# Selective attention followed by a hard-swish feed-forward: loading of the first pair, two mask tables and the second half's bias sums moved

## The chip, the cores and the metric

The kernel runs on one core of one Trainium2 chip. A core has a matrix engine (TensorE, PE in the profile, with its weight loads shown apart as PEld), a vector engine (VectorE, DVE), an activation engine (ScalarE, ACT), a general engine (GpSimd, POOL) and a queue engine (SyncE, SP). Each runs its own list of instructions in order, and they wait for each other through semaphores. Transfers between the main memory and the core's memory are issued by SP, ACT or POOL; only POOL's change the number type on the way.

The metric is the device time of one execution in microseconds, the median of several runs. Lower is better.

## The reference

Shapes: 8 batches, 8 heads, 576 tokens, head size 64, feed-forward width 2048.

```
scores = scale * q @ k^T                          # scale 1/8, per head
cum    = cumsum(max(s, 0))                        # s: one number per head and token
bias   = -(cum[:, None] - cum[None, :])
scores = where(causal, -1e9, scores + min(bias, 0))
attn   = softmax(scores);   x = attn @ v          # heads side by side: 4608 x 512
h      = x @ w_in                                 # 512 x 2048
g      = h * clip(h + 3, 0, 6) / 6
out    = g @ w_out                                # 2048 x 512, float32
```

## The kernel before, in words

**Pairs and slots.** The 64 heads are worked off as 32 pairs of one batch. The main loop runs over the pair `p`; a *slot* is one pass, and slots are counted here from 0, as `p` is. In slot `p` PE computes the scores of pair `p`, ACT the exponentials (L335), PE the product with V (`av`, L386), DVE the division (`norm`, L408 and L409); a transpose brings the result into `xT`. Between these pieces stand calls of `group()`: each puts in one group of four 512-column matmuls of the feed-forward, either of its first product (`m1`, L452, followed by ACT's relu L467 and DVE's L468) or of its second (`m2`, L479, after every fourth of which DVE L495 scales the output block). Up to slot 13 a string, `plan`, says which; after that first and second products alternate while inputs allow. Groups begin in slot 4.

**How q and k arrive.** PE needs them in fp16 with the head size on the partitions. There are two ways. For pairs that are not *flat* (1 to 10), POOL issues a transfer that converts to fp16 on the way (L115, one for q and one for k), PE transposes it (L234), and four copies put it in place (L251; for k the even tokens' copy is ACT's). For flat pairs (0, and 11 on) SP or ACT issues a plain float32 transfer (L120), an engine casts it (`cast_qk`, L183), and it is transposed by PE (pair 0: L227, copies L211) or by a transposing transfer (pairs 11 on: L266 in SP's queue, copies L211 by DVE). V comes as float32 by three transfers in SP's queue (L131, L135), and POOL casts it (L187, L188).

**Bias.** The bias of a pair is added inside the score product: four extra rows (64 to 67) of the transposed q and k hold the running sums of `s`, split in fp16 parts. The sums of the first 32 heads are made at the start (`cum1` to `cum6`: a DVE scan L645, casts and subtractions), those of the other 32 heads later. `load_aug(p)` (L143) moves the rows of pair `p` in place, two small transfers. Pair 0 can't wait for that: DVE's `pick` (L668) makes its rows, and PE adds them by extra products (L282, L327).

**Masks.** Pairs 0 to 7 are masked by a product with a table `shut`. From pair 8 on rows 68 to 127 of the transposed q and k hold a *staircase* table, and DVE takes a minimum (L337, L369). There are four q/k buffers; each gets its table once (`set_stair`, L594, one copy for each head): POOL does it in slots 6 and 7, ACT at the beginning of slots 8 and 9, for the pairs 10 and 11.

**Order.** The order is written out by hand: what stands first in the program is first on its engine. Buffers: scores two banks, `ph` two banks, P three, V raw two, V cast three, q/k four. POOL's and SP's transfers each take one of eight semaphores in turn, so that one of them can wait until the eighth before it has landed.

**The start.** SP and ACT issue the loads of `s`, SP issues q of pair 0 and then its V, ACT issues k. PE runs 16 products on zeros (L606, `warm`, NWARM), ACT casts q and k, PE transposes them, ACT and DVE copy them, PE runs 4 more products on zeros, and the scores of pair 0 begin. POOL builds the identity and `shut`, issues pair 1's transfers, then pair 2's, casts V of pair 0, issues pair 3's.

Of the kernel before, what the change touches and what calls it, by code (L numbers as in the profile page):

```python
# [18 lines left out]
def kernel(  # L19
# [10 lines left out]
    nc = tc.nc  # L30
# [7 lines left out]
    NP = NHEADS // 2  # L38
# [10 lines left out]
    NVRAW = 2  # L49
    VW = 66  # L50
    NROW = 1
    NWARM = (16, 4)

# [47 lines left out]
    toks = {}  # L103

    def flat(p):
        return p < 1 or p >= NPE

    def load_qk(p, i, eng=nc.sync):
        b, h0 = p // PPB, 2 * (p % PPB)
        src = (q, k)[i][b, h0 : h0 + 2]  # L110
        if not flat(p):
            if not i:
                tok = work.tile([128, 24 * D], F16, tag="tok", bufs=4, name="tok")
                toks[p] = tok[0:96].rearrange("p (i h e d) -> p i h e d", i=2, h=2, e=6)
            nc.gpsimd.dma_start(  # L115
                out=toks[p][:, i].rearrange("p h e d -> p h (e d)"),
                in_=src.rearrange("h (p e) d -> p h (e d)", e=6),
            )
        else:
            eng.dma_start(  # L120
                out=raws[p % NRAW].rearrange("p (i t d) -> p i t d", i=2, t=9)[:, i],
                in_=src.rearrange("h s d -> (h s) d").rearrange(
                    "(t p) d -> p t d", p=128
                ),
            )
# [40 lines left out]
    def fill(eng, ap, value):  # L166

        word = np.array([value, value], np.float16).view(np.float32)[0]
        eng.memset(ap.bitcast(F32), float(word))
# [387 lines left out]
    def load_s(n, engs):  # L557
# [3 lines left out]
            eng.dma_start(out=C[n][32 * r : 32 * (r + 1)], in_=heads)  # L561

    load_s(0, (nc.sync, nc.scalar, nc.sync, nc.scalar))
    load_qk(0, 0)
    load_qk(0, 1, nc.scalar)
    nc.scalar.preload_act_table_set("natural_log_exp_and_others")
    load_v(0, nc.sync)
    fill(nc.gpsimd, ident, 0.0)
# [6 lines left out]
        base=0,  # L575
        channel_multiplier=-1,
    )
    fill(nc.gpsimd, shut, 0.0)
    for c in (slice(0, 512), slice(512, 640)):
        w = 128 if c.start == 0 else 64  # L580
# [8 lines left out]
            channel_multiplier=-1,  # L589
        )  # L590

    def set_stair(i, copy):
        for hh in range(2):
            copy(  # L594
                out=qks[i][64:128, hh, :, 64 * hh : 64 * hh + 640].rearrange(
                    "p i (t c) -> p i t c", c=128
                ),
                in_=stair_sb[64:128, :, None, :].to_broadcast([64, 2, 5, 128]),
            )
# [15 lines left out]
    nc.vector.memset(bias3, 3.0)  # L615
    fill(nc.gpsimd, rows_of[0][:, 0, :], 1.0)
    fill(nc.gpsimd, rows_of[0][:, 1, SEQ:640], 0.0)
    fill(nc.gpsimd, qks[0][64:68, :, :, :], 0.0)
    for i in range(2):
        load_qk(1, i)  # L620
    for i in range(NQK):
# [11 lines left out]
        op=ALU.add,  # L633
    )
    nc.vector.tensor_scalar_mul(out=ident2, in0=ident, scalar1=2.0)

    def cum1(n, eng):
        C["p"] = work.tile([128, SEQ], F32, tag="spos", bufs=1, name="spos")
# [4 lines left out]
    def cum2(n):  # L643
        C["c"] = work.tile([128, SEQ], F32, tag="c8", bufs=1, name="c8")
        nc.vector.tensor_tensor_scan(  # L645
            out=C["c"], data0=one.to_broadcast([128, SEQ]), data1=C["p"], initial=0.0, op0=ALU.mult, op1=ALU.add
        )
# [5 lines left out]
    def cum4(n, eng):  # L653
        C["r"] = work.tile([128, SEQ], F32, tag="s_all", bufs=1, name="r1")
        hi = rows_of[n][64:128, 1, 0:SEQ]
        eng.tensor_tensor(
            out=C["r"][64:128], in0=C["c"][64:128], in1=hi, op=ALU.subtract
        )
# [28 lines left out]
        out=C["p"][:, 304:SEQ], in_=C[0][:, 304:SEQ], func=AF.Relu, scale=8.0  # L687
    )
    cum2(0)
    nc.scalar.copy(out=rows_of[0][0:32, 0, 0:SEQ], in_=C["c"][0:32])  # L690
    cast_qk(0, nc.scalar.copy)
    cum3(0, V)
    cum4(0, V)
    cum5(0, V)
    cum6(0, V)
    pick(0)
    transpose(0, 0, (nc.scalar.copy,) * 2)
    transpose(0, 1)
    warm(NWARM[1])
    for g in range(1, 2 * NROW):  # L700
        pick(g)
    load_aug(1, nc.sync)
    load_v(1, nc.sync)
    load_aug(2, nc.sync)
    for i in range(2):
# [12 lines left out]
    for p in range(NP):  # L718
        nxt = p + 1 < NP
        if NPE <= p + 3 < NP:  # L720
            for i in range(2):
                load_qk(p + 3, i)
        def qk_ahead():
            if PPB < p + 3 < NPE:
                for i in range(2):
                    load_qk(p + 3, i)

        if p == 1:
            load_aug(4, nc.gpsimd)
        elif p == 2:  # L730
            load_w_in(0)
            cast_v(2)
            qk_ahead()
            load_aug(5, nc.gpsimd)
        elif p == 3:
            cast_v(3)
            load_w_in(1)
            qk_ahead()
            load_aug(6, nc.gpsimd)
            cast_v(4)  # L740
        elif p:
            qk_ahead()
            if NPE <= p + 2 < NP:
                cast_qk(p + 2)
                crossbar_qk(p + 2)
            for fn, c in {
                4: ((I, 2),),
                5: ((I, 3),),
                6: ((U, 0), (U, 1), (U, 2), (U, 3)),
                7: ((U, 4), (U, 5), (U, 6), (U, 7)),  # L750
            }.get(p, ()):
                fn(c)
            if nxt:
                cast_v(p + 1)
            if p in (6, 7):
                set_stair((p + 2) % NQK, nc.gpsimd.tensor_copy)
            elif p in (8, 9):
                set_stair((p + 2) % NQK, nc.scalar.copy)
            if p == 4:
                load_aug(7, nc.gpsimd)  # L760
            elif 5 < p < NP - 2:
                load_aug(p + 2, nc.gpsimd)
        if p and p + 2 < NP:
            load_v(p + 2, nc.sync)
        if p == 2:
            nc.sync.dma_start(out=stair_sb, in_=stair_dram.ap())
        if p == 9:
            load_s(1, (nc.sync,) * 4)
            fill(nc.gpsimd, rows_of[1][:, 0, :], 1.0)
        if p == 10:  # L770
            cum1(1, nc.gpsimd)
        if p == 11:
            cum2(1)
            nc.gpsimd.tensor_copy(out=rows_of[1][0:32, 0, 0:SEQ], in_=C["c"][0:32])
        if p == 12:
            cum3(1, nc.gpsimd)
            cum4(1, nc.gpsimd)
        if p == 13:
            cum5(1, nc.gpsimd)
            cum6(1, nc.gpsimd)  # L780

        if p == NPROD + 1:
            x_done[0] = NPROD

        def get(i):
            if p + 1 < NPE:
                transpose(p + 1, i)
            elif nxt:
                spread(p + 1, i)

        if p < PPB:
            scores(p, 0, 0)
            scores(p, 0, 1)
            get(0)
            scores(p, 0, 2)
            corner(p)
            if p:
                av(p - 1, 1, 0)
                av(p - 1, 1, 1)
                norm(p - 1, 1)  # L800
            get(1)
            scores(p, 1, 0)
            scores(p, 1, 1)
            av(p, 0, 0)
            scores(p, 1, 2)
            if p:
                transpose_x(p - 1)
            av(p, 0, 1)
            norm(p, 0)
            continue  # L810

        if p == PPB:
            early[0] = False
            scores(p, 0, 0)
            av(p - 1, 1, 0)
            av(p - 1, 1, 1)
            norm(p - 1, 1)
            m1_begin(0, 0, NKC - 1)
            scores(p, 0, 1)
            transpose_x(p - 1)  # L820
            m1_begin(0, 1, NKC - 1)
            pt = transpose_in(p + 1, 0)
            transpose_out(p + 1, 0, pt, pars=(0,))
            group()
            transpose_out(p + 1, 0, pt, pars=(1,))
            scores(p, 0, 2)
            group()
        else:
            if p == NPROD:
                nc.vector.tensor_scalar(  # L830
                    out=masks, in0=shut, scalar1=65504.0, scalar2=None, op0=ALU.add
                )
            scores(p, 0, 0)
            get(0)
            group()
            scores(p, 0, 1)
            av(p - 1, 1, 0)
            if p >= NPE - 1:
                get(1)
            group()  # L840
            scores(p, 0, 2)
            av(p - 1, 1, 1)
            norm(p - 1, 1)
            group()
        corner(p)
        group()
        if p > NPE:
            x_done[0] = p - 1
        if p == PPB:
            get(1)  # L850
            av(p, 0, 0)
        scores(p, 1, 0)
        if PPB < p < NPROD:
            get(1)
        group()
        if NPROD <= p < NPE - 1:
            get(1)
        scores(p, 1, 1)
        if p != PPB:
            av(p, 0, 0)  # L860
        if PPB < p < NPROD:
            transpose_x(p - 1)
        elif p >= NPROD:
            crossbar_x(p - 1)
        group()
        scores(p, 1, 2)
        group()
        av(p, 0, 1)
        norm(p, 0)
        group()  # L870
# [3 lines left out]
    group()  # L874
    av(p, 1, 1)
    norm(p, 1)
    group()
    group()
    transpose_x(p)
# [31 lines left out]
```

## Time and profile before

| | |
|---|---|
| Median of 5 runs | 359.68 us (359.47 to 361.41) |
| The profiled execution | 360.13 us, of which its span (first to last instruction) is 358.3 |
| Granted TensorE clock | 0.999 |
| PE busy | 347.0 us, 97% of the span |
| DVE, ACT, POOL busy | 251.4, 224.9, 127.5 us |
| DMA engines, mean busy | about 1.0 to 1.2 in the stretch to 65 us, 0.1 to 0.2 after 260 us |

The profile names an instruction by engine, line, operation and operands. A row of the timeline gives start, duration, then what runs and how often; in brackets the engine's idle time before it and what ended that. Matmuls overlap, so that a row's duration is longer than the time to the next start: a group of four 512-column matmuls is shown as 1.03 us, and the next row starts 0.86 us after it. What a wait costs PE is read from starts.

### The profile page before, as it was taken

What the parts mean: (1) busy time and instruction counts of PE and PEld (TensorE: products, weight loads), DVE (VectorE), ACT (ScalarE), POOL (GpSimd) and SP (SyncE); (2) the same over time, 40 slices, a digit from 0 to 9 for tenths busy, and PEclk for the clock granted to TensorE, in tenths of its full rate; (3) what the DMA queues carried; (4) which work ended last, traced back from release to release, by engine and by line L of the source; (5) the groups of instructions that cost most, each with busy time, mean ns of one, the idle gap of its engine ahead of it and who ended that gap; (6) DMA issues with size and microseconds to landing.
All of it is one profiled execution on the core that took longest, in us unless ns stands there. A gap on an engine that the chain in (4) does not pass through costs nothing.

```text
span 358.3 us, 7729 instructions
## 1 busy us (share of the span) xinstructions
PE 347.0 (97%) x2920; PEld 191.7 (54%) x2920; DVE 251.4 (70%) x541; ACT 224.9 (63%) x390; POOL 127.5 (36%) x219
## 2 busy tenths in 40 slices
PE   8999998899999999999999999999999999999995
PEld 3776665555555555555555555555555444444442
DVE  7897997697998777786768776767665544545531
ACT  4897888788677666666666666666665344333410
POOL 8575976654674433434233524342000000000000
PEclk9999999999999999999999999999999999999999
DMA  9899999989999996979698959899320101101111
GB/s 172 142 196 175 181 195 199 186 186 177 208 209 170 234 186 162 202 168 183 158 164 197 202 130 203 155 208 148 72 77 20 59 2 59 59 2 59 59 58 63
DMA packets 146991, 50.88 MB, mean 142 GB/s; under 512 B 133624, under 2 KB 141992, under 8 KB 146952
## 3 DMA queue, kind: packets, MB, share of 16 engines
q1 hardware_dynamic: 135304, 42.13, 59.8%
q0 software_dynamic: 10240, 7.67, 13.9%
q10 hardware_dynamic: 1408, 0.57, 0.7%
q8 instruction: 23, 0.38, 0.4%
q14 instruction: 16, 0.13, 0.1%
HBM read 37.36 MB, written 9.44 MB: 131 GB/s over the span
## 4 chain that ended last, share of the span: by engine, by line
PE 84%; DVE 6%; DMA 4%; ACT 3%; issue 1%; POOL 1%; ACTq 0%; SPq 0%; DVEq 0%; POOLq 0%
PE po L479 33%; PE ph L452 32%; PE O L386 7%; PE S L316 7%; PE S L305 3%; DMA vraw<-in_v_dram 3%; ACT qk L594 1%; DVE gT L468 1%; DVE qk L251 1%; ACT P L335 1%; DMA s_all<-in_s_dram 1%; PE pt L234 1%; DVE qk L211 1%; ACT tr L467 1%; DVE x L409 1%
## 5 line engine op out<-in xcount | busy, mean ns | idle before, releaser
L468 DVE SCALAR_TENSOR_TENSOR gT<-tr,ph 128x512 f16<-128x512 f32 x144 | 98.9, 687 | 78.0 <-ACT tr L467 76.5
L452 PE MATMUL ph<-xT,w_in_sb 128*128 128x512 f16 x576 | 148.2, 379 | 0.3 <-DVE gT L468 0.2
L479 PE MATMUL po<-w_out_sb,gT 128*128 128x512 f16 x576 | 145.8, 379 | 0.3 <-DMA w_out_sb<-in_moe_w_out_dram 0.3
L467 ACT ACTIVATE tr<-ph,bias 128x512 f32<-128x512 f32 x144 | 99.0, 687 | 73.0 <-PE ph L452 71.5
L335 ACT ACTIVATE P<-S 128x512 f16<-128x512 f32 x192 | 111.5, 596 | 39.1 <-PE S L305 21.6
L452 PEld LDWEIGHTS <-w_in_sb 128*128 128x128 f16 x576 | 51.8, 97 | 44.7 <-issue 0.5
L479 PEld LDWEIGHTS <-gT 128*128 128x128 f16 x576 | 50.2, 98 | 46.5 <-issue 0.8
L316 PE MATMUL S<-qk 68*128 68x448 f16 (+3 forms) x256 | 48.9, 272 | 0.9 <-ACT P L335 0.9
L183 POOL CAST tok<-raw 128x576 f16<-128x576 f32 x42 | 28.2, 673 | 58.7 <-DMA raw<-in_q_dram 47.2
L386 PE MATMUL O<-va,P 128*128 128x65 f16 x896 | 47.8, 193 | 0.6 <-POOL va L187 0.6
L386 PEld LDWEIGHTS <-P 128*128 128x128 f16 x896 | 39.4, 97 | 14.4 <-issue 0.7
L187 POOL CAST va<-vraw 128x512 f16<-128x512 f32 x32 | 20.4, 638 | 56.7 <-DMA vraw<-in_v_dram 42.5
L316 PEld LDWEIGHTS <-qk 68*128 68x128 f16 x256 | 23.7, 98 | 24.9 <-issue 1.4
L143 POOL DMA_DIRECT2D qk<-rows_of x56 | 33.3, 597 | 3.5 <-PE S L305 2.5
L409 DVE TENSOR_TENSOR x<-O,rl 128x320 f16<-128x320 f32 x64 | 31.5, 492 | 2.2
L211 DVE COPY qk<-jt 64x768 f16<-64x768 f16 x84 | 31.3, 372 | 1.2
L495 DVE TENSOR_SCALAR ob<-po 128x512 f32<-128x512 f32 (+1 forms) x36 | 24.4, 678 | 9.5 <-PE po L479 8.9
L337 DVE TENSOR_TENSOR P<-P,shut 128x512 f16<-128x512 f16 x48 | 24.5, 511 | 5.6 <-ACT P L335 5.5
L305 PEld LDWEIGHTS <-qk 128*128 128x128 f16 (+1 forms) x256 | 18.9, 98 | 13.7 <-DVE qk L251 1.2
L251 DVE COPY qk<-pt 64x576 f16<-64x576 f16 x30 | 24.1, 804 | 3.0 <-PE pt L234 1.3
L305 PE MATMUL S<-qk 128*128 128x128 f16 (+1 forms) x256 | 25.0, 219 | 1.2 <-DVE rl L408 0.7
L386 PE MATMUL O<-va,PC 128*128 128x65 f16 x64 | 12.4, 193 | 0.8 <-DVE PC L369 0.8
(72 smaller groups left out, 174.4 us busy)
## 6 DMA issues: line engine op xcount, KB each, us to landing
out_dram<-ob SPq DMA_DIRECT2D x35, 256.0 KB, 2.0
vraw<-in_v_dram SPq DMA_DIRECT2D x64, 128.0 KB, 3.3
raw<-in_q_dram SPq DMA_DIRECT2D x22, 288.0 KB, 4.0
raw<-in_k_dram SPq DMA_DIRECT2D x21, 288.0 KB, 4.3
w_in_sb<-in_moe_w_in_dram POOLq DMA_DIRECT2D x4, 512.0 KB, 9.4
w_out_sb<-in_moe_w_out_dram POOLq DMA_DIRECT2D x8, 256.0 KB, 9.5
tok<-in_q_dram POOLq DMA_DIRECT2D x10, 144.0 KB, 5.2
tok<-in_k_dram POOLq DMA_DIRECT2D x10, 144.0 KB, 5.4
```

What stands on the lines that cost most here:

```text
L143: eng.dma_start(out=qks[p % NQK][64:68, hh, :, 64 * hh : 64 * hh + SEQ], in_=rows_of[g // 32].rearrange("(r g) i t -> g r i t", g=32)[g % ...
L183: copy(out=toks[p][:, c], in_=raws[p % NRAW][:, c])
L211: copies[par](out=qk[0:64, :, i, 128 * par : 128 * par + 256 * n].rearrange("p h (s two c) -> p h s two c", two=2, c=128)[:, :, :, 0, :], ...
L305: mm(S[:, c], lhsT=kT[rows, c], rhs=qT[rows, c], start=(j == 0 and not by_product), stop=(j == 3),)
L316: mm(S[:, c : c + w], lhsT=kT[0:68, 128 * j : 128 * (j + 1)], rhs=qT[0:68, 128 * (j + 1) : SEQ], start=(c == 0), stop=(c != 0 and p >= NROW),)
L335: nc.scalar.activation(out=pt[:, c], in_=S, func=AF.Exp, scale=0.125)
L386: mm(o[:, i, :], lhsT=lhsT, rhs=va[:, hh, j, 0:65], **kw)
L409: nc.vector.tensor_tensor(out=X[p][:, :, hh, :], in0=o[:, :, 0:64], in1=rl.to_broadcast([128, 5, 64]), op=ALU.mult,)
L452: mm(ph, lhsT=w_in_sb[:, kc, ft * 128 : (ft + 1) * 128], rhs=xT[:, kc, n * 512 : (n + 1) * 512], start=(kc == 0), stop=(kc == NKC - 1),)
L467: nc.scalar.activation(out=tr, in_=ph, func=AF.Relu, bias=bias3[:, 0:1])
L468: nc.vector.scalar_tensor_tensor(out=gTs[n][:, ft, :], in0=tr, scalar=6.0, in1=ph, op0=ALU.min, op1=ALU.mult)
L479: mm(po, lhsT=gTs[n][:, ft, t4 * 128 : (t4 + 1) * 128], rhs=w_out_sb[:, ft, :], start=(ft == 0), stop=(ft == NFT - 1),)
```

## The change

It has these parts.

1. Pair 0 is no longer flat: its q and k come by POOL's converting transfers, issued after the identity is built and before `shut`. The float32 transfers (one in SP's queue, one in ACT's) and ACT's two casts go. Its transposes are now twelve of 96 columns (L234) and its copies four of L251: ACT makes both of q and the even one of k, DVE the odd one of k. In ACT's order q's copies stand before the cast of the bias row (L690, now L692), k's behind it; in DVE's order k's copy stands between `pick(0)` and `pick(1)`.
2. NWARM goes from (16, 4) to (12, 10).
3. `load_aug(1)` moves from SP's queue to POOL's, ahead of pair 2's transfers and the cast of pair 0's V.
4. Half of a clearing of four partitions (L169 on `qk`) goes from POOL to DVE.
5. ACT's staircases of slots 8 and 9 are done one head at a time: the first after the corner, the second after the last scores of the slot. `load_aug(10)` and `load_aug(11)` go behind the second.
6. The second bias sums: the loads of `s` go from slot 9 to 12, `cum1` from 10 to 13, and `cum2` (the DVE scan) to `cum6`, in slots 11 to 13 before, all to slot 14, followed there by `load_aug(16)`.
7. One more `group()` before the transpose of the last pair.

```
-    NWARM = (16, 4)
+    NWARM = (12, 10)
     def flat(p):
-        return p < 1 or p >= NPE
+        return p >= NPE
     load_s(0, (nc.sync, nc.scalar, nc.sync, nc.scalar))
-    load_qk(0, 0)
-    load_qk(0, 1, nc.scalar)
     nc.scalar.preload_act_table_set("natural_log_exp_and_others")
     load_v(0, nc.sync)
...
+    for i in range(2):
+        load_qk(0, i)
     fill(nc.gpsimd, shut, 0.0)
...
-    def set_stair(i, copy):
-        for hh in range(2):
+    def set_stair(i, copy, heads=(0, 1)):
+        for hh in heads:
...
-    fill(nc.gpsimd, qks[0][64:68, :, :, :], 0.0)
+    fill(nc.gpsimd, qks[0][64:68, 1, :, :], 0.0)
...
     nc.vector.tensor_scalar_mul(out=ident2, in0=ident, scalar1=2.0)
+    fill(nc.vector, qks[0][64:68, 0, :, :], 0.0)
...
     cum2(0)
+    transpose(0, 0, (nc.scalar.copy,) * 2)
     nc.scalar.copy(out=rows_of[0][0:32, 0, 0:SEQ], in_=C["c"][0:32])
-    cast_qk(0, nc.scalar.copy)
     cum3(0, V)
     cum4(0, V)
+    pt = transpose_in(0, 1)
+    transpose_out(0, 1, pt, pars=(0,))
     cum5(0, V)
     cum6(0, V)
     pick(0)
-    transpose(0, 0, (nc.scalar.copy,) * 2)
-    transpose(0, 1)
+    transpose_out(0, 1, pt, pars=(1,))
     warm(NWARM[1])
     for g in range(1, 2 * NROW):
         pick(g)
-    load_aug(1, nc.sync)
+    load_aug(1, nc.gpsimd)
...
             if p in (6, 7):
                 set_stair((p + 2) % NQK, nc.gpsimd.tensor_copy)
-            elif p in (8, 9):
-                set_stair((p + 2) % NQK, nc.scalar.copy)
             if p == 4:
                 load_aug(7, nc.gpsimd)
-            elif 5 < p < NP - 2:
+            elif p in (6, 7) or 9 < p < NP - 2 and p != 14:
                 load_aug(p + 2, nc.gpsimd)
...
-        if p == 9:
+        if p == 12:
             load_s(1, (nc.sync,) * 4)
             fill(nc.gpsimd, rows_of[1][:, 0, :], 1.0)
-        if p == 10:
+        if p == 13:
             cum1(1, nc.gpsimd)
-        if p == 11:
+        if p == 14:
             cum2(1)
             nc.gpsimd.tensor_copy(out=rows_of[1][0:32, 0, 0:SEQ], in_=C["c"][0:32])
-        if p == 12:
             cum3(1, nc.gpsimd)
             cum4(1, nc.gpsimd)
-        if p == 13:
             cum5(1, nc.gpsimd)
             cum6(1, nc.gpsimd)
+            load_aug(16, nc.gpsimd)
...
         corner(p)
+        if p in (8, 9):
+            set_stair((p + 2) % NQK, nc.scalar.copy, (0,))
         group()
...
         scores(p, 1, 2)
         group()
+        if p in (8, 9):
+            set_stair((p + 2) % NQK, nc.scalar.copy, (1,))
+            load_aug(p + 2, nc.gpsimd)
         av(p, 0, 1)
         norm(p, 0)
         group()
...
     av(p, 1, 1)
     norm(p, 1)
     group()
+    group()
     group()
     transpose_x(p)
```

More of the change, by code (lines that the diff above doesn't have):

```diff
@@ L51 @@
     NROW = 1
-    NWARM = (16, 4)
+    NWARM = (12, 10)
     grp = (np.arange(128) * 61 // 128)[None, :]
@@ L105, in flat @@
     def flat(p):
-        return p < 1 or p >= NPE
+        return p >= NPE
     def load_qk(p, i, eng=nc.sync):
@@ L563 @@
     load_s(0, (nc.sync, nc.scalar, nc.sync, nc.scalar))
-    load_qk(0, 0)
-    load_qk(0, 1, nc.scalar)
     nc.scalar.preload_act_table_set("natural_log_exp_and_others")
@@ L577 @@
     )
+    for i in range(2):
+        load_qk(0, i)
     fill(nc.gpsimd, shut, 0.0)
@@ L590, with set_stair @@
         )
-    def set_stair(i, copy):
-        for hh in range(2):
+    def set_stair(i, copy, heads=(0, 1)):
+        for hh in heads:
             copy(
@@ L617 @@
     fill(nc.gpsimd, rows_of[0][:, 1, SEQ:640], 0.0)
-    fill(nc.gpsimd, qks[0][64:68, :, :, :], 0.0)
+    fill(nc.gpsimd, qks[0][64:68, 1, :, :], 0.0)
     for i in range(2):
@@ L635 @@
     nc.vector.tensor_scalar_mul(out=ident2, in0=ident, scalar1=2.0)
+    fill(nc.vector, qks[0][64:68, 0, :, :], 0.0)
     def cum1(n, eng):
@@ L689 @@
     cum2(0)
+    transpose(0, 0, (nc.scalar.copy,) * 2)
     nc.scalar.copy(out=rows_of[0][0:32, 0, 0:SEQ], in_=C["c"][0:32])
-    cast_qk(0, nc.scalar.copy)
     cum3(0, V)
     cum4(0, V)
+    pt = transpose_in(0, 1)
+    transpose_out(0, 1, pt, pars=(0,))
     cum5(0, V)
@@ L696 @@
     pick(0)
-    transpose(0, 0, (nc.scalar.copy,) * 2)
-    transpose(0, 1)
+    transpose_out(0, 1, pt, pars=(1,))
     warm(NWARM[1])
@@ L701 @@
         pick(g)
-    load_aug(1, nc.sync)
+    load_aug(1, nc.gpsimd)
     load_v(1, nc.sync)
@@ L756 @@
                 set_stair((p + 2) % NQK, nc.gpsimd.tensor_copy)
-            elif p in (8, 9):
-                set_stair((p + 2) % NQK, nc.scalar.copy)
             if p == 4:
                 load_aug(7, nc.gpsimd)
-            elif 5 < p < NP - 2:
+            elif p in (6, 7) or 9 < p < NP - 2 and p != 14:
                 load_aug(p + 2, nc.gpsimd)
@@ L766 @@
             nc.sync.dma_start(out=stair_sb, in_=stair_dram.ap())
-        if p == 9:
+        if p == 12:
             load_s(1, (nc.sync,) * 4)
             fill(nc.gpsimd, rows_of[1][:, 0, :], 1.0)
-        if p == 10:
+        if p == 13:
             cum1(1, nc.gpsimd)
-        if p == 11:
+        if p == 14:
             cum2(1)
             nc.gpsimd.tensor_copy(out=rows_of[1][0:32, 0, 0:SEQ], in_=C["c"][0:32])
-        if p == 12:
             cum3(1, nc.gpsimd)
             cum4(1, nc.gpsimd)
-        if p == 13:
             cum5(1, nc.gpsimd)
             cum6(1, nc.gpsimd)
+            load_aug(16, nc.gpsimd)
         if p == NPROD + 1:
@@ L845 @@
         corner(p)
+        if p in (8, 9):
+            set_stair((p + 2) % NQK, nc.scalar.copy, (0,))
         group()
@@ L867 @@
         group()
+        if p in (8, 9):
+            set_stair((p + 2) % NQK, nc.scalar.copy, (1,))
+            load_aug(p + 2, nc.gpsimd)
         av(p, 0, 1)
@@ L876 @@
     norm(p, 1)
+    group()
     group()
```

## The prediction

> **What bounds the kernel now.** I read the page first, then PE's waits, then the timeline around each.
>
> ```profile
> PE 347.0 (97%) x2920; PEld 191.7 (54%) x2920; DVE 251.4 (70%) x541; ACT 224.9 (63%) x390; POOL 127.5 (36%) x219
> PE 84%; DVE 6%; DMA 4%; ACT 3%; issue 1%; POOL 1%; ACTq 0%; SPq 0%; DVEq 0%; POOLq 0%
> ```
>
> PE is the bound, and the chain that ended last is PE for 84%. A gain can only come from PE's waits and from the start:
>
> ```profile
> PE S L316 <- ACT P L335: 0.9, 1, 0.9
> PE O L386 <- DVE PC L369: 0.8, 1, 0.8
> PE S L305 <- DVE rl L408: 0.7, 1, 0.7
> PE O L386 <- POOL va L187: 0.6, 1, 0.6
> PE po L479 <- DMA w_out_sb<-in_moe_w_out_dram: 0.3, 1, 0.3
> PE S L305 <- DVE qk L251: 0.3, 1, 0.3
> ```
>
> A matmul's drawn end hides a part of each wait, so I price them by starts, against the same pair of rows elsewhere: slot 4, V of pair 4, 30.68 to 31.73 where 24.25 to 24.50 is usual: 0.80 lost; slot 8, 60.04 to 61.39 against 78.23 to 78.48: 1.10; the w_out wait 0.49 (two matmuls take 0.92, not 0.43); scores of pair 9, 67.17 to 68.03 against 71.34 to 71.37: 0.83; scores of pair 10, 76.44 to 76.91: 0.44; slot 11, 90.84 to 91.97 against 95.52 to 95.70: 0.95; the last pair's transpose, 276.22 to 277.44 where a group takes 0.86: 0.36. Together 5.0 us: more is not to be had behind the start. The rows:
>
> ```profile
> 4.34 0.81 POOL L115 DMA_DIRECT2D tok<-in_q_dram  x1
> 8.62 0.60 DVE L668 TENSOR_SCALAR w_out_sb<-rows_of,sel 128x576 f16<-128x576 f16 x1
> 9.25 1.01 DVE L211 COPY qk<-pt 64x768 f16<-64x768 f16 x2
> 10.32 0.34 PE L305 MATMUL S<-qk 68*128 68x128 f16 x3 [0.22 <-DVE qk L211]
> 14.86 0.61 POOL L187 CAST va<-vraw 128x512 f16<-128x512 f32 x1 [4.28 <-DMA vraw<-in_v_dram]
> 31.73 0.41 PE L386 MATMUL O<-va,P 128*128 128x65 f16 x8 [0.63 <-POOL va L187]
> ...
> 58.31 2.41 ACT L594 COPY qk<-stair_sb 64x1280 f16<-64x1280 f16 x2
> 61.39 0.38 PE L316 MATMUL S<-qk 68*128 68x320 f16 x2 [0.95 <-ACT P L335]
> 66.56 0.59 PE L479 MATMUL po<-w_out_sb,gT 128*128 128x512 f16 x2 [0.32 <-DMA w_out_sb<-in_moe_w_out_dram]
> 68.03 0.38 PE L305 MATMUL S<-qk 128*128 128x128 f16 x4 [0.67 <-DVE rl L408]
> 76.91 0.40 PE L305 MATMUL S<-qk 128*128 128x128 f16 x4 [0.28 <-DVE qk L251]
> ...
> 86.36 1.35 DVE L645 TENSOR_TENSOR_SCAN c<-one,spos 128x576 f32<-128x576 f32 x1
> 91.97 0.20 PE L386 MATMUL O<-va,PC 128*128 128x65 f16 x1 [0.79 <-DVE PC L369]
> ```
>
> The first scores hang on DVE's queue; V's cast idled for 4.28 us for a load; the staircase on ACT stopped PE in slot 8; two waits on transfers follow it; the scan in slot 11 made DVE late.
>
> **The change part by part.** Shifts are PE's place against before.
>
> *Start.* POOL can issue q at 1.28 (identity done at 1.25) and k at 2.1 (0.81 and 0.68 each). Pair 1's transfers took 4.2 and 4.0 from issue to landing while the DMA engines were full (share 1.34 to 1.36 from 4 to 7 us), so q lands at 5.5, k at 6.1. PE's 12 products start 0.427 apart from 1.19: done at 6.3, and this decides. Transposes 0.42, so ACT starts at 6.7: q's two copies 1.6, bias row 0.67 (9.0), k's even copy 0.8 (9.8); DVE's odd copy, which waits for that, 0.81; scores at 10.6, against 10.32: +0.3. `pick(0)`, which now waits for ACT's row until 9.0, ends at 9.65 and fits before. PE's ten products (2.15) end before 9.1. The two casts (1.24) and two plain issues go, but ACT was not last. Bounds: DVE's own chain (8.62 + 0.60 + 0.81 = 10.0) gives -0.3; a landing as slow as the slowest later pair's (10.2) gives +3.9. I take +0.3, by the nearest rows in time. The half clearing on DVE (1.44 for all on POOL, so about 0.7) fits DVE's 1.13 idle before `s`.
>
> *V and POOL's queue.* SP no longer waits with pair 1's V behind the bias rows (8.75), so that V is there early, and POOL doesn't idle 4.28. From the row at 9.0 POOL has `load_aug(1)` 1.2, pair 2's transfers 1.3, V's cast 1.3 (done at 12.8; `av` needs it at 13.2 + 0.3), pair 3's 1.3, V's cast 0.9, pair 4's 1.25, two bias issues 1.2: the first w_in load goes out at 17.4, not 18.07. Pair 2's q lands at 10.2 + 3.4 = 13.6, needed at 14.7 + 0.3. Pair 4's V is held by the full DMA engines behind that load (share 1.1 to 1.25 from 18 to 32), so it lands some 0.65 earlier than 30.9; PE reaches it at 31.1 + 0.3 = 31.4 and waits no more: shift -0.3. Bounds: -0.8 (start unchanged, wait gone) to the start's whole loss.
>
> *Slot 8.* No staircase ahead of the exponentials: 1.10 gone. But the last w_out load (issued 57.74) landed 8.8 later, at 66.5, just when PE went on; pair 9's bias rows, behind it in POOL's queue (61.89, landing 6.0 later), at 67.9, and PE started pair 9 at 68.03. I put that wait down to them, not to the DVE row named. The DMA engines are full from 41 to 65 (share 1.2), so these landings move only with POOL's earlier work: 0.3 to 0.65, I take 0.45. Pair 9 starts at 67.6: the 1.10 is swallowed. Shift -0.45; -1.55 if the stream follows PE.
>
> *Slots 9 and 10.* The staircase no longer delays ACT's first exponential of pair 9 (69.36 becomes 68.4); losses of 0.2 twice (68.95, 72.46) go. But a half (1.25) now stands between the corner's exponential and pair 9's second head: ACT 72.6 to 73.8, then exponential, relu and k's copy (74.42 before) at 74.8 to 75.6, DVE's copy to 76.45, pair 10 at 76.5: shift -0.4. The other half stands at 77.2 to 78.4, ahead of pair 10's first exponential (77.34 before, now 78.35): its score banks come free late, for PE 0.1 and 0.25. Shift -0.1 after slot 10. Bounds: +1.5, if both halves of slot 9 reach PE almost whole (2 x 1.25 less 0.9), and -0.8, if neither does. The moved `load_aug(10)` and `(11)` now wait for ACT at about 67 and 78.4; behind them POOL holds the casts of pair 11's and 12's q and k, whose transposing transfers SP issued at 71.2 and 80.65. The second cast then ends near 81: a little late, covered until DVE reads it (88.3 before).
>
> *Slot 11.* The scan (1.35) goes, and the cast of POOL beside DVE's copy: -0.95, to -1.05. Bounds 0 to -0.95.
>
> *Slot 14.* There the scan is added, and five sums on POOL (0.68, 0.68, 1.28, 0.67, 1.28 in before's rows) with a clearing, waiting for the scan, and then `load_aug(16)`; behind them pair 17's cast. Pair 16 has a whole slot for it.
>
> ```profile
> 92.50:100.30 7.80, 7.80 (x74) 4.48 (x73) 7.64 (x17) 5.49 (x10) 5.66 (x10) 1.00 1.05 186
> 100.30:109.00 8.70, 8.70 (x82) 5.10 (x81) 8.51 (x19) 6.05 (x11) 6.22 (x9) 1.00 1.16 223
> 109.00:117.50 8.50, 8.50 (x79) 4.81 (x77) 6.26 (x15) 5.72 (x11) 3.28 (x6) 1.00 1.09 167
> ```
>
> These are slots 12 to 14: length, then busy PE, PEld, DVE, ACT, POOL. DVE has 2.2 of 8.5 us free in slot 14, more than 1.35; in slots 12 and 13, with the sums, it was full and PE lost nothing. I take +0.15; bounds 0 and 0.95, as in slot 11.
>
> DVE's two copies at 78.74 took 0.65 with POOL quiet, and at 89.81, beside POOL's cast at 89.73, 1.12. [...]
>
> *`s` loads and `cum1`* in slots 12 and 13: SP's four issues (2.04) and POOL's 2.15 move; POOL's casts waited 47.2 us in total for raw loads, so nothing for PE; if that cover is gone a cast is 2 us late, against a slot's slack. *Last `group()`*: 0.86 of ready work before the transpose; -0.35 (0 to -0.36).
>
> Sum: -0.1 - 0.95 + 0.15 - 0.35 = -1.25. The profiled execution took 360.13, 0.45 above the median 359.68: 358.9 in its terms, 358.4 as a median. A difference under about 0.3% (1.1 us) I count as none.
>
> **The rivals.**
>
> 1. *Slot 8's 1.10 is kept*, because the transfer stream runs earlier with PE: -1.1 more, 357.3. For: w_out's issues wait for landings that began with work PE releases. Against: share 1.2 for 24 us.
> 2. *Nothing is gained*: the halves reach PE in slots 9 and 10 (+0.6 on my figure) and the scan's loss only moves to slot 14 (+0.8): 359.8. For: DVE had no idle time from 70 to 77. Against: DVE's room in slot 14.
> 3. *Slower: pair 11's bias rows come too late.* Issued at 78.4 instead of 69.9, needed by its first scores at 84.4 less the shift. Landings of such rows took 2.4 to 8.4; over 6 it decides, and at 8.4 costs 2.4: 360.8. Against: 3.3 to 3.6 at that place before.
> 4. *Slower: pair 0 lands late*, as do later pairs with other loads beside them (8.4 at 19.65). k would be there at 10.5, scores 2.3 later; slot 4's wait and slot 8's spare 1.1 take up part if the transfers keep their time, else 2 remain: about 360.7. It decides from a landing of 6 or more.
>
> **How the numbers follow.** My forecast 0.48, rival 1 0.12, rival 2 0.20, rivals 3 and 4 0.10 each. The forecast lies just beyond the bound, with some 0.08 of its 0.48 within it. Faster: 0.40 + 0.12 = 0.52; same: 0.20 + 0.08 = 0.28, of which rivals' milder cases take no more; slower 0.20. The range goes from 356.8 (rival 1 with the start at -0.3) to 361.0 (rivals 3 and 4); for the likeliest case alone 357.6 to 359.2.
>
> **What would show it.** Scores of pair 0 at 10.6 with ACT's L251 from 6.7; POOL without an idle 4 us before pair 1's V; no POOL wait at `av` of slot 4; no ACT wait in slot 8 but a longer w_out wait and pair 9 at 67 to 68; an L305 wait at pair 10 and an ACT one in slot 10; no wait on L369 in slot 11; DVE full in slot 14. Wrong would be: transposes of pair 0 past 7, a wait on `qk` at pair 11, or a wait over 1 us in slot 14.

## The result: 0.7% slower

The changed kernel took 362.07 us as the median of 28 runs (360.74 to 366.01), against 359.91 for the kernel before (52 runs, 359.28 to 364.49). The medians lie 0.6% apart; the ratio of 1.0074, 95% interval 1.0053 to 1.0095, is that of the means (362.99 and 360.33), which the long runs raise. Ratios leave out runs more than 1.5% above the fastest of the same kernel; that concerns two of r1's twelve below. The profiled run took 360.74, span 358.9, against 360.13 and 358.3 before. So two things have to be explained: the profile is 0.6 us longer where 1.25 less was forecast, and the median lies another 1.3 above the profile.

The page and the waits of the changed kernel, in us in total, times, longest:

```profile
PE 346.6 (97%) x2924; PEld 192.0 (53%) x2924; DVE 250.8 (70%) x541; ACT 224.4 (63%) x389; POOL 128.8 (36%) x223
...
POOL qk L143 <- ACT qk L594: 12.7, 4, 4.8
PE ph L452 <- DVE gT L468: 4.2, 2, 2.6
PE S L305 <- DVE qk L251: 0.6, 1, 0.6
```

The waits of before on L335 in slot 8, L369 (slot 11), L187 (slot 4) and the `w_out` loads are gone from this list. Two new ones have come: PE waits 4.2 us for `gT`, in two places, and POOL stands 12.7 us behind ScalarE's staircases with bias rows to issue (L143).

First the kernel before in slots 9 and 10, POOL's casts and bias rows and DVE's masking (L337):

```profile
66.83 0.66 POOL L183 CAST tok<-raw 128x576 f16<-128x576 f32 x1 [1.75 <-DMA raw<-in_q_dram]
69.99 0.42 DVE L337 TENSOR_TENSOR P<-P,shut 128x512 f16<-128x512 f16 x1 [1.48 <-ACT P L335]
73.39 0.66 POOL L183 CAST tok<-raw 128x576 f16<-128x576 f32 x1 [1.96 <-DMA raw<-in_q_dram]
77.90 1.28 POOL L143 DMA_DIRECT2D qk<-rows_of  x2
```

The timeline of the changed kernel around slots 9 and 10 (start, length, engine, operation, in brackets the idle time before it and what ended it):

```profile
64.27 1.33 SPq L436 DMA_TRANSPOSE xT<-x  x1
65.78 0.38 PE L305 MATMUL S<-qk 128*128 128x128 f16 x4
67.35 0.57 POOL L143 DMA_DIRECT2D qk<-rows_of  x1 [3.10 <-ACT qk L594]
67.70 1.84 DVE L337 TENSOR_TENSOR P<-P,shut 128x512 f16<-128x512 f16 x1 [0.68 <-ACT P L335]
67.92 1.28 POOL L183 CAST tok<-raw 128x576 f16<-128x576 f32 x2
71.11 0.69 DVE L468 SCALAR_TENSOR_TENSOR gT<-tr,ph 128x512 f16<-128x512 f32 x1
71.85 1.02 PE L452 MATMUL ph<-xT,w_in_sb 128*128 128x512 f16 x4 [1.55 <-DVE gT L468]
...
77.85 0.57 POOL L143 DMA_DIRECT2D qk<-rows_of  x1 [4.79 <-ACT qk L594]
78.21 1.84 DVE L337 TENSOR_TENSOR P<-P,shut 128x512 f16<-128x512 f16 x1 [0.58 <-ACT P L335]
78.42 1.28 POOL L183 CAST tok<-raw 128x576 f16<-128x576 f32 x2
79.63 0.89 POOL L187 CAST va<-vraw 128x512 f16<-128x512 f32 x1
79.97 2.16 DVE L211 COPY qk<-jt 64x768 f16<-64x768 f16 x2
80.71 1.22 POOL L143 DMA_DIRECT2D qk<-rows_of  x2
82.91 1.02 PE L452 MATMUL ph<-xT,w_in_sb 128*128 128x512 f16 x4 [2.61 <-DVE gT L468]
```

Read each half from the top. POOL issues the second head's bias rows as soon as ScalarE has finished its staircase, and its casts follow at once. DVE's masking (L337) runs at that moment and takes 1.84 us; its next one, at 73.67, takes 0.42. In slot 10 the copies behind it (L211) take 2.16 instead of 0.65, beside POOL's cast of V and the next bias issues. `gT`, which stands behind them in DVE's queue, is late, and PE stops.

Where the time went is seen best from PE's place at the first scores of each pair, after against before: pair 0 10.50 against 10.32 (+0.2), pair 9 65.78 against 68.03 (-2.3), pair 10 75.60 against 76.91 (-1.3), pair 11 86.40 against 84.42 (+2.0), pair 12 93.90 against 92.88 (+1.0), and the end +0.6. The changed kernel is 2.3 us ahead at pair 9, gains 1.4 behind pair 11, and loses 4.2 in slots 9 and 10. Not all of the 2.3 is the change's: r11 below, the kernel before with one transfer moved, comes to pair 9 at 66.65, 1.4 earlier than the profile of before, and still takes 360.38.

The runs do not scatter evenly. Ten of the 28 took 360.7 to 361.1 at a granted clock of 0.998 or 0.999; six 362.0 to 362.3 at 0.993 to 0.995; five 364.0 to 364.9 at 0.994 or 0.995; seven 365.5 to 366.0 at 0.989 to 0.991. The profile is one of the ten, and the median lies in the second group.

### The profile page after: what moved, and what is told of

The parts are those of the page before. It is cut to its first block, busy times and chain, and to the rows that moved or that the text cites. A ratio compares the mean times of both kernels' runs of the same rounds, so it can differ in the third digit from the quotient of the medians.

```text
span 358.9 us, 7734 instructions
## 1 busy us (share of the span) xinstructions
PE 346.6 (97%) x2924; PEld 192.0 (53%) x2924; DVE 250.8 (70%) x541; ACT 224.4 (63%) x389; POOL 128.8 (36%) x223
## 4 chain that ended last, share of the span: by engine, by line
PE 90%; DVE 5%; ACT 3%; issue 1%; ACTq 0%
PE po L479 34%; PE ph L452 33%; PE O L386 7%; PE S L316 7%; PE S L305 4%; DVE qk L251 2%; PE W L606 1%; PE pt L234 1%; DVE P L337 1%; ACT P L335 1%; PE ptx L423 1%; DVE gT L468 1%; PE S L298 1%; DVE qk L211 1%; DVE x L409 1%
## 5 line engine op out<-in xcount | busy, mean ns | idle before, releaser
L335 ACT ACTIVATE P<-S 128x512 f16<-128x512 f32 x192 | 111.3, 595 | 38.4 <-PE S L305 20.4
L143 POOL DMA_DIRECT2D qk<-rows_of x58 | 33.9, 586 | 15.8 <-ACT qk L594 12.7
L187 POOL CAST va<-vraw 128x512 f16<-128x512 f32 x32 | 20.8, 651 | 51.7 <-DMA vraw<-in_v_dram 40.1
L211 DVE COPY qk<-jt 64x768 f16<-64x768 f16 x84 | 30.5, 363 | 1.2
L337 DVE TENSOR_TENSOR P<-P,shut 128x512 f16<-128x512 f16 x48 | 25.2, 525 | 6.0 <-ACT P L335 5.9
L251 DVE COPY qk<-pt 64x576 f16<-64x576 f16 x31 | 25.0, 805 | 3.1 <-PE pt L234 1.6
```

Of the source, the lines that this page charges most:

```text
L143: eng.dma_start(out=qks[p % NQK][64:68, hh, :, 64 * hh : 64 * hh + SEQ], in_=rows_of[g // 32].rearrange("(r g) i t -> g r i t", g=32)[g % ...
L211: copies[par](out=qk[0:64, :, i, 128 * par : 128 * par + 256 * n].rearrange("p h (s two c) -> p h s two c", two=2, c=128)[:, :, :, 0, :], ...
L251: copies[par](out=bass.AP(to.tensor, to.offset, [list(to.ap[0]), [2 * SPAD + 64, 2], [6, 96], [2, 3]],), in_=pt[64 * par : 64 * par + 64, ...
L335: nc.scalar.activation(out=pt[:, c], in_=S, func=AF.Exp, scale=0.125)
```

## The experiments

Theory A: the bias rows of pairs 10 and 11 (part 5), put behind ScalarE's second half, hold POOL's queue; the casts queued behind them then run against DVE's own operations, which makes `gT` late. Rival B: the halves on ScalarE do it themselves. For the scatter: theory C, PE's stalls let the clock drop; C1, the shorter warm-up at the start does; C2, formed after the first four runs, a transfer lands late in some runs.

| run | median, us | runs | range | ratio to before, 95% interval |
|---|---|---|---|---|
| changed kernel | 362.07 | 28 | 360.74 to 366.01 | 1.0074 (1.0053, 1.0095) |
| r1, rows behind the casts | 357.62 | 12 | 357.01 to 362.80 | 0.9953 (0.9923, 0.9984) |
| r2, part 5 undone | 358.78 | 12 | 357.89 to 360.87 | 0.9971 (0.9953, 0.9989) |
| r3, part 5 alone | 363.13 | 7 | 361.20 to 364.96 | 1.0084 (1.0053, 1.0116) |
| r4, start alone | 360.14 | 12 | 359.45 to 361.46 | 0.9993 (0.9973, 1.0013) |
| r5, casts twice | 361.51 | 10 | 360.06 to 365.20 | 1.0045 (1.0005, 1.0084) |
| r9, r1 and x ahead of V | 357.80 | 6 | 357.06 to 358.59 | 0.9931 (0.9907, 0.9956) |
| r10, changed, x ahead of V | 361.61 | 12 | 360.69 to 363.00 | 1.0049 (1.0031, 1.0067) |
| r11, before, x ahead of V | 360.33 | 10 | 359.26 to 360.44 | 1.0001 (0.9986, 1.0016) |
| r12, r9 again | 358.10 | 7 | 357.24 to 358.71 | 0.9963 (0.9950, 0.9975) |

**r1: only the place of the bias rows.**

```diff
             if nxt:
                 cast_v(p + 1)
+            if p in (9, 10):
+                load_aug(p + 1, nc.gpsimd)
...
             set_stair((p + 2) % NQK, nc.scalar.copy, (1,))
-            load_aug(p + 2, nc.gpsimd)
```

> The changed kernel, with the bias rows of pairs 10 and 11 issued on POOL behind the casts of slots 9 and 10, instead of behind ScalarE's second half and ahead of those casts. ScalarE's halves stay where they are. [...] Rival B (the halves themselves, 1.25 each ahead of ScalarE's own work, make gT late): the waits stay over 1 us each and the time stays at 360 to 361. On the scatter of the changed kernel's runs (360.7 to 366 with granted clocks of 0.999 to 0.989): theory C (PE's stalls of 1.7 and 2.8 us let the clock drop) has it gone here, all runs within 1.5 us at 0.997 or more; rival C1 (the start with 12 warm products instead of 16 does it) has it stay.

The profiled run took 357.15, 3.6 us less than the changed kernel's. Its timeline in the same two slots:

```profile
63.55 0.67 POOL L183 CAST tok<-raw 128x576 f16<-128x576 f32 x1 [2.15 <-DMA raw<-in_q_dram]
66.76 1.15 POOL L143 DMA_DIRECT2D qk<-rows_of  x2
67.46 0.42 DVE L337 TENSOR_TENSOR P<-P,shut 128x512 f16<-128x512 f16 x1 [0.68 <-ACT P L335]
70.73 0.66 POOL L183 CAST tok<-raw 128x576 f16<-128x576 f32 x1 [2.82 <-DMA raw<-in_q_dram]
...
77.09 1.72 POOL L143 DMA_DIRECT2D qk<-rows_of  x3 [1.50 <-ACT qk L594]
77.45 0.43 DVE L337 TENSOR_TENSOR P<-P,shut 128x512 f16<-128x512 f16 x1 [0.58 <-ACT P L335]
77.80 0.65 DVE L211 COPY qk<-jt 64x768 f16<-64x768 f16 x2
78.81 1.48 POOL L183 CAST tok<-raw 128x576 f16<-128x576 f32 x2
```

L337 is back at 0.42 and 0.43, also at 77.45, where POOL was issuing bias rows, and so are the copies at 77.80: these issues alone slow neither. The casts of pairs 11 and 12 start when their data land, at 63.55 and 70.73 (the waits on `raw`), where the changed kernel has them at 67.92 and 78.42. PE waits for no `gT`. The halves are where they were, so B falls. But 4 of the 12 runs took 361.4 to 362.8 at 0.994 or 0.995: with the stalls gone the scatter is not, so C in its first form doesn't hold for these. No profile caught one of the four.

**r2: part 5 undone. r3: part 5 alone. r4: parts 1 to 4 alone** (r4 is r2 with parts 6 and 7 undone as well).

```diff
+            elif p in (8, 9):                                  # r2
+                set_stair((p + 2) % NQK, nc.scalar.copy)
-            elif p in (6, 7) or 9 < p < NP - 2 and p != 14:
+            elif 5 < p < NP - 2 and p != 14:
                 load_aug(p + 2, nc.gpsimd)
...
-        if p in (8, 9):
-            set_stair((p + 2) % NQK, nc.scalar.copy, (0,))     # and the second half with its rows
```

> The changed kernel with part 5 undone: both heads of the staircase on ScalarE at the beginning of slots 8 and 9, the bias rows of pairs 10 and 11 in their old place in POOL's queue. All else stays changed. Theories A and B: the gT waits of slots 9 and 10 are gone, slot 8's 1.1 us for ScalarE is back; the start, slot 4, slot 11 and the tail keep +0.2, -0.3, -0.95 and -0.35: 358.0 to 358.8 as a median. If instead part 5 is not what cost (some other part is), it stays at 360.7 or more. Theory C: no scatter by the granted clock. C1: scatter as in the changed kernel, since the start is the changed one.

> The kernel before with part 5 alone: halves of the staircase and the bias rows of pairs 10 and 11 behind the second half. Theories A and B: gT waits of some 1.5 and 2.6 us in slots 9 and 10 on the old start, less slot 8's 1.1 to 2: a profile at full clock of 361 to 362.5. Theory C: runs scatter up to 366 with granted clocks down to 0.99. C1: no such scatter, because the start is the old one.

> The kernel before with the start alone (pair 0 by POOL's converting transfers, 12 and 10 warm products, pair 1's bias rows on POOL, the half clearing on VectorE). By the prediction's steps: +0.2 to +0.3 at the first scores, and -0.3 after slot 4: 359.6 as a median, within 0.5. Theory C: no more scatter by the clock than the kernel before has. C1: scatter to 365 or 366, as in the changed kernel.

r2 took 358.78, so part 5 as made costs the changed kernel 3.3 us of its median (3.7 by the ratios). Alone on the kernel before it cost 3.0 (363.13): the `gT` waits are there (2.5 us together), L337 took 1.53 and 1.84, and 2 of 7 runs had clocks of 0.995 and 0.992. Two more took 363.1 and 363.6 at a clock of 1.000; no profile shows why. r4 stands where the kernel before stands, with all 12 clocks at 0.997 or more: C1 falls. r2 less r4, parts 6 and 7, is -1.36. In r4 PE is 1.44 ahead of before at pair 9 (66.59 against 68.03) and only 0.75 ahead at pair 10 (76.16 against 76.91): PE now comes to slot 9 before ScalarE has finished pair 11's staircase. That lead is not the start's. r11, with the old start, has 66.65 and 76.22; what r4's and r11's profiles share is an earlier last `w_out` issue, 53.73 and 54.75, against 57.74 in the profile of before. r11's rows:

```profile
54.75 0.70 POOL L159 DMA_DIRECT2D w_out_sb<-in_moe_w_out_dram  x1 [1.06 <-DMA w_out_sb<-in_moe_w_out_dram]
66.65 0.38 PE L305 MATMUL S<-qk 128*128 128x128 f16 x4
```

**r5: POOL's casts of pairs 11 and 12 issued twice.**

```diff
-            copy(out=toks[p][:, c], in_=raws[p % NRAW][:, c])
+            for _ in range(2 if p in (11, 12) else 1):
+                copy(out=toks[p][:, c], in_=raws[p % NRAW][:, c])
```

> The changed kernel with POOL's two casts of pairs 11 and 12 each issued twice (the same values once more), so that the burst behind the held bias rows is about 1.28 us longer in each of slots 9 and 10. Theory A (VectorE's L337 and L211 are held for as long as POOL's burst lasts): L337 grows from 1.84 to about 3.1 us in both slots or hands the rest to the next copy, the waits of L452 for gT grow from 1.55 and 2.61 by 0.9 to 1.3 each, and the profile takes 362.5 to 363.5. Rival B (the halves on ScalarE make gT late; POOL's casts are only beside it): POOL has the room (127 of 360 us busy), the waits stay within 0.3 us and the time at 360.5 to 361.

This went against A's numbers. Five of the ten runs took 360.06 to 360.58, below the changed kernel's shortest, 360.74. The profiled run is the longest, 365.20: PE waited 2.64 us in it for pair 7's `x` in slot 9, as in r6 and r7 below, so it is held against these two. Its timeline has (lines one further down in this file):

```profile
82.48 1.18 DVE L338 TENSOR_TENSOR P<-P,shut 128x512 f16<-128x512 f16 x1 [0.58 <-ACT P L336]
82.69 2.96 POOL L184 CAST tok<-raw 128x576 f16<-128x576 f32 x4
```

Twice the casts held the masking for less time, 1.18 instead of the changed kernel's 1.84, and the casts themselves took 0.74 each instead of 0.64. The `gT` waits of slot 10 came to 2.6 us (1.27 and 1.35), as in r6 and r7 (2.61, one wait each), and did not grow by 0.9 to 1.3. So DVE is not held for as long as POOL's burst lasts (2.96 here, beside a masking of 1.18). A keeps its core (late rows, and casts that now meet DVE); the size of the loss does not follow from the length of the casts, and what sets it stays open.

**r6 and r7: the changed kernel again, r8: r1 again**, with no edit, to catch a long run in a profile.

> The changed kernel once more, for a profile of one of its longer runs (of 28 runs 18 took 362 us or more, at granted clocks of 0.989 to 0.995). If the profile falls there: theory C says that PE's stalls in slots 9 and 10 (1.7 and 2.8 us) are followed by a stretch at a lower granted clock, which costs 1.3 to 5 us; rival C1 places that stretch at the start, before 10 us; rival C2 has a transfer land late (pair 11's bias rows or another), so that PE waits some microseconds more than in the profile of 360.74, and the clock drops behind that. In a run near 360.8 nothing of this is to be seen.

> The changed kernel a third time, for the same reason and with the same expectations: a stretch at a lower clock behind the stalls of slots 9 and 10 (theory C), at the start (C1), or behind an added wait for a transfer (C2).

> The kernel with the bias rows of pairs 10 and 11 behind the casts once more. It has no stall over 1 us behind the start, and yet 4 of its 12 runs took 361.4 to 362.8 at 0.994 or 0.995, the others 357.0 to 357.8. Theory C in its form so far is wrong for those: either the start does it (C1) or a transfer that lands late in some runs (C2). If this profile falls among the long ones it shows the place; else it takes 357.0 to 357.8 with the waits of the first look.

They took 366.02, 365.05 and 357.36: the first two are long. The timeline of r6, SP's queue and PE:

```profile
57.67 5.49 SPq L131 DMA_DIRECT2D vraw<-in_v_dram  x2
63.26 1.96 SPq L135 DMA_DIRECT2D vraw<-in_v_dram  x1
65.32 1.32 SPq L436 DMA_TRANSPOSE xT<-x  x1
69.60 0.38 PE L452 MATMUL ph<-xT,w_in_sb 128*128 128x512 f16 x1 [2.60 <-DMA xT<-x]
```

Pair 7's transposing transfer of `x` (`crossbar_x`) stands in SP's queue behind pair 10's V loads. Here it went out at 65.32 and landed 4.2 us later; PE came to it 2.6 early. r7 has the same wait (issued 65.83, 4.3). In the first profile of the changed kernel it went out at 64.27 and landed in 2.7, just as PE needed it. In the profile of before it went out at 66.66 and landed at 69.4, and PE lost about 0.2 on it. The whole queue is later in the long runs: the last `w_out` load went out at 56.29 and 56.45, against 54.84 in the first profile and 55.25 and 54.62 in those of r1 and r8. The kernel before has 57.74 in its own profile and 54.75 in r11's, which differs in no step ahead of it: this stream moves by 3 us from one execution to the next.

The windows of r6 right after that wait (length, busy PE, PEld, DVE, ACT, POOL, granted clock, DMA share, GB/s):

```profile
68.00:72.00 4.00, 2.40 (x16) 1.09 (x16) 3.44 (x4) 1.17 (x2) 1.94 (x4) 0.79 0.89 209
72.00:76.00 4.00, 4.00 (x41) 2.51 (x40) 2.20 (x5) 2.27 (x4) 0.00 (x0) 0.79 1.00 227
```

The clock dropped behind the stall: 0.79 for 8 us, which is 1.7 us less than at 1.00 (8 x 0.21). After the `gT` wait of slot 10 it dropped again (0.92 and 0.65 from 84 to 92, again 1.7), in r7 after that one only (0.81 and 0.77, 1.7). By this estimate one such dip takes 0.0047 off a run's mean clock (1.7 of 360); r7, with one, has 0.995, and r6, with two, 0.990. So I read 0.994 as one and 0.990 as two.

**r9 to r12: SP issues x ahead of V in slot 8.** r9 (and r12) on r1, r10 on the changed kernel, r11 on the kernel before.

```diff
-        if p and p + 2 < NP:
+        if p and p + 2 < NP and p != 8:
             load_v(p + 2, nc.sync)
...
             crossbar_x(p - 1)
+            if p == 8:
+                load_v(10, nc.sync)
```

> The kernel with the bias rows of pairs 10 and 11 behind the casts, and besides, in slot 8, SP issues pair 7's transposing transfer of x ahead of pair 10's V loads instead of behind them. In the long profiles of the changed kernel PE waited 2.6 us in slot 9 for that x (issued at 65.3 and 65.8, landed 4.2 and 4.3 later), in the short ones it did not (64.3 and 64.0, 2.7 later). Theory C2 (that transfer, held in SP's queue by V's loads, is what parts long runs from short ones): x goes out by 63, no run waits for it, all 12 runs take 356.7 to 358.0 and none shows 0.996 or less. Rivals C (stalls in slots 9 and 10) and C1 (start): 3 to 5 of 12 runs still at 361 to 363.

> The changed kernel with that one move in SP's queue alone. Theory C2: the wait for x goes from all runs, and the gT waits of slots 9 and 10 stay, so that all runs take what the first profile took, 360.4 to 361.3, the median 1.0 to 1.4 below the changed kernel's 362.07. If the gT stalls alone (1.7 and 2.8 us) lower the clock in some runs, a part of the runs stays at 362 to 364 (theory C). Rival C1: over half of the runs stay at 362 to 366.

> The kernel before with that one move in SP's queue alone. There PE comes to x at 69.4, and x had landed by 69.4 (issued at 66.7): no gain in the usual run, 359.4 to 360.2 as a median, and fewer of the rare runs over 361.5. If V of pair 10 comes late behind x, a wait of PE for va in slot 10 shows, and the time rises by it.

> The kernel with the bias rows behind the casts and pair 7's x ahead of pair 10's V once more, since its first look had only 6 runs, and 4 of 12 runs of the kernel without the move in SP's queue took 361.4 to 362.8. Theory C2: no run above 359, none at a granted clock under 0.996, the median 357.0 to 358.2. If the long runs came from something else, about a third of these runs takes 361 or more.

In r10 no run is above 363.0, where 12 of the changed kernel's 28 were at 364 or more, which fits that these were the late `x`; the changed kernel was not run beside r10, and r6 and r7 ran on another chip than r10. What is left parts in two: six runs at 360.7 to 361.1 (0.998 or 0.999), five at 362.1 to 362.9 (0.994 or 0.995), and one at 363.0 with 0.998, which stays unexplained, like two runs of r5 (362.4 and 363.6 at 1.000). So theory C holds for its part: the `gT` stalls alone went with a lower mean clock in about half of the runs (0.993 to 0.995 in six of the changed kernel's 16 without a late `x` and in five of r10's 12), for 1.1 us in the changed kernel and 1.4 in r10, by the medians of the groups. The two together give the groups of the result: no dip 360.9; one dip 362.05; late `x` and one dip 364 to 364.9; late `x` and two dips 365.5 to 366. My expected range for r10 (360.4 to 361.3, median 361.1 at most) held for half of its runs.

The timeline of r12, whose `x` went out 1.8 us earlier than the changed kernel's, and whose PE passed it without a wait:

```profile
62.51 1.32 SPq L436 DMA_TRANSPOSE xT<-x  x1
66.07 1.03 PE L452 MATMUL ph<-xT,w_in_sb 128*128 128x512 f16 x4
```

All 13 runs of r9 and r12 took 357.06 to 358.71 at 0.997 or more. With a third of them long, as in r1, that would come about in 1 case of 200 (0.667 to the 13th is 0.005). This version is faster than both kernels, at 0.9931 and 0.9963 of before in two sets of runs; r1's median is as good, but four of its 12 runs were long, and none of these 13. r9's profile shows that the late stream did occur among them: the last `w_out` issue stood at 57.05, later than in r6 and r7, and PE waited for `w_out` (0.9 in two places) but not for `x`; it took 358.59.

```profile
57.05 0.70 POOL L159 DMA_DIRECT2D w_out_sb<-in_moe_w_out_dram  x1 [0.94 <-DMA w_out_sb<-in_moe_w_out_dram]
63.82 1.99 SPq L436 DMA_TRANSPOSE xT<-x  x1
```

In r11 the move changes nothing (1.0001), as was to be expected where PE lost only 0.2 on `x`.

## Why the prediction was wrong, point by point

The forecast was 358.4 with 0.52 for faster; it came out slower, at 362.07, above the range.

- *Start* (+0.3): right. Pair 0's scores at 10.50 (10.6 said), transposes of q at 6.20 (6.3). The +3.9 of a late landing did not come.
- *V and POOL's queue*: right in the steps, not in the gain. V's cast of pair 1 at 14.10 without the 4.28 of idle time, the first w_in at 17.31 (17.4 said), no wait at `av` of slot 4. But the 0.3 that PE was to be ahead didn't come: pair 5's scores start at 35.15 against 35.02 and pair 8's at 58.45 against 58.47. Two waits for ScalarE's L335 in slot 4 (0.2 each by the waits) stood behind the one removed. And that one, priced at 0.80, was one execution's: r3 and r11, with the old start, have no wait at that `av` but the same two for L335.
- *Slot 8*: wrong in size. I let the 1.10 be swallowed by `w_out` and bias rows, since "these landings move only with POOL's earlier work: 0.3 to 0.65". The last `w_out` issue was 2.9 us earlier, and pair 9 started at 65.78, not 67.6. Rival 1, at 0.12, had the number, the 1.10 kept; its mechanism, a stream that runs earlier with PE, is not shown, since the stream's place was one execution's, not the kernel's. r11, with the old start and the old staircase but its last `w_out` issue at 54.75, starts pair 9 at 66.65: of the 2.25 us, 1.4 came with the early stream and 0.9 with the change, near 1.10 less the start's 0.2.
- *Slots 9 and 10*: here the prediction failed. I had 0.35 lost from pair 9 to the end of slot 10; it was 4.2 (20.62 us from pair 9 to pair 11, against 16.39). Against r11, which comes early to pair 9 as well, it is 3.4 (17.25), against r1, which differs in the place of the rows alone, 3.3 (17.35). I saw the bias rows waiting for ScalarE "at about 67 and 78.4" and the casts behind them late, both right to within 0.6 us, and wrote them off as "a little late, covered until DVE reads it". That asks only who waits for the casts' data. It should also have asked what runs on DVE at their new time. r1 shows it: the same work, with the rows behind the casts, has no `gT` wait and takes 3.6 us less in the profile. My upper bound for these slots, +1.5, priced ScalarE's halves, which r1 shows to be harmless to `gT`; what they do cost there is a wait of 0.8 us for L335 before pair 10's scores.
- *DVE beside POOL*: I weighed what DVE loses beside POOL's casts (1.12 for copies that take 0.65) in slots 11 and 14 alone, and slot 14 lost nothing. The larger loss came earlier, in slots 9 and 10, where L337 took 1.84 beside the casts, against 0.42 and 0.43 in r1. The trace does not tell what decides it: the rows at 67.70 and 67.92 have DVE's start ahead, and yet DVE lost 1.42, and r5's doubled casts cost it less. One reading was wrong: at 78.74 POOL was not quiet but issuing bias rows (77.90 to 79.18), and the copies took 0.65 beside them.
- *Slot 11* (-0.95): right. From pair 11 to pair 12 the changed kernel gains 0.96 on before.
- *Slot 14* (+0.15, bounds 0 and 0.95): nothing lost. DVE is fuller than in before, PE without a gap:

```profile
109.00:117.50 8.50, 8.50 (x80) 4.79 (x77) 8.29 (x17) 5.85 (x11) 5.54 (x9) 1.00 1.01 180
```

- *Tail* (-0.35): right, +1.0 at pair 12 becomes +0.6 at the end. Slots 11, 14 and the tail were -1.15 together in the forecast; r2 less r4 measured -1.36.
- *The median*: I carried the profile's sum to the median by the offset of before (-0.45). That left out that a new stall can change the clock: 18 of 28 runs had, by their clocks, at least one dip, and 12, by their times, the late `x`. None of my signs for "wrong" was the one that came: pair 0 was in time, no pair waited for bias rows, slot 14 was clean.

## What to carry to other kernels

When an issue that waits is put ahead in an in-order queue, what is behind it is not only late: it runs at another time, beside other work (here POOL's casts, at 67.92 and 78.42 instead of r1's 63.55 and 70.73). Look up what the other engine does then, and price that, not just who waits for the result. And where a stall is removed, name the transfer that PE reaches next and how far it lies ahead in several executions, not in one: here PE's coming 2.3 us earlier to pair 9 made a load's order in SP's queue decide over another 2 to 5 us. Price the waits of the kernel before from several executions as well: its profile and r11's lay 1.4 us apart at pair 9 and 0.25 at the end.

## What the runs showed of the hardware

- A wait of 2.6 us in PE's stream was followed by a dip of the granted clock in some executions (0.79 for 8 us in r6; 1.7 us of full clock, at each dip of r6 and r7) and not in others: in r6 after both waits of 2.6, in r7 after the second only, in the first profile not after its one of 2.6, and by their clocks in five of r10's 12 runs. What decides between them is not shown.
- The same transposing transfer took 2.7 us to land in most profiles, but 4.2 or 4.3 in r5 to r7, and 4.2 also in r9 and 3.5 in r10, where no V load stood ahead of it. V's loads set when it goes out; how long it takes did not follow from them.
- One stream of loads (the last `w_out` issue) lay between 53.7 and 57.1 us in the eleven profiles with the changed start, and at 54.8, 56.6 and 57.7 in the three with the old one. Waits for `w_out` or `x` in slots 8 and 9 went with an issue at 56.3 or later; the profiles with 55.5 or earlier had none there.
